# Halved z1 weights kept in DRAM, longer runs of P.V and other PSUM banks in a fused attention and gMLP kernel

## The chip, the cores and the metric

The kernel runs on one core of a Trainium2 chip. The metric is the device time of one execution in microseconds; lower is better. Given are the median of three runs of the kernel before and one profiled execution of it.

## The reference

Two branches read the same normalised input (2048 tokens, 576 features); their product is added to the input.

```python
def _A_ref(x, wqkv, wo):                # 32 heads of 18, causal window of 256
    q, k, v = ...
    scores = einsum("bhqd,bhkd->bhqk", q, k) * Dh ** -0.5
    mask = (i - j >= 0) & (i - j < 256)
    p = softmax(where(mask, scores, -1e9))
    return einsum("bhqk,bhkd->bhqd", p, v)... @ wo

def _B_ref(x, w_in, w_sp, b_sp, w_out): # Fh = 2304
    z = gelu(x @ w_in)
    z1, z2 = z[..., :Fh], layernorm(z[..., Fh:])
    g = einsum("ts,bsf->btf", w_sp, z2) + b_sp[None, :, None]
    return (z1 * g) @ w_out

xn = layernorm(x)
out = x + _A_ref(xn, ...) * silu(_B_ref(xn, ...))
```

## The kernel before, in words

Everything is float32, but TensorE multiplies in a rounded format (float32r). So an operand is *halved*: a high part is a copy by ScalarE (ACT) into float32r, a low part is the rest, by a subtraction on VectorE (DVE) or GpSimd (POOL). A product then takes three matmuls: high by high, high by low, low by high. The 576 input features are nine blocks of 64 rows, so two matmuls of 64 rows each work side by side in the upper and the lower half of TensorE's array; they write the PSUM banks `ma` and `mb`.

The program passes through these stages:

- q, k and v (0 to 195 us of the span). q and k go to `st_d` in DRAM, v to `v_d`.
- z2 (195 to 425 us): 6 pieces of 384 columns (`pc`) by 8 steps of two token tiles (`q`). A step is 27 matmuls in each half; then ACT takes both banks through a gelu into `zt` (four tiles), which SP stores to `z2_d`. Beside it run two generators, advanced once a step: the next piece's weights (fetched by L892 into the tiles named `z1wh` and `z1wl`, halved into `z2w` or into the `att` slots), and `sp_combos`, which loads four blocks of the spatial weights (`a`, L850), makes sums on POOL (L858 to L862) and stores them to `sc_d` (L867).
- The heads (425 to 854 us), and with them z1 = x @ w_z1. For each unit of four heads and half of the tokens there are 32 *maxima* (`max_item`: a matmul of L603 into a bank `sp`, then one DVE operation of L606, which adds the mask `band` and takes the largest score of each query; it is there before the exponentials), and *scores* per key block (`scores`: a matmul of L741 into a bank `tps`, an exponential by ACT into `pt`, and a POOL operation, L753 or L756, that clears what the mask forbids). `pv` multiplies `pt` by v, four heads side by side in parts of 32 columns of the array (L769). What is left of TensorE's time is filled with z1: 18 blocks of 128 columns by two halves by two banks of 27 matmuls (L685).
- The rest of z1 and the product with `wo` (854 to 945 us), the spatial product by a scheme of seven products (945 to 1634), the output product (1634 to 1846).

All DMAs are issued by SP, in one queue. In the heads the order of every engine is written out at build time by a planner: the program keeps a clock with planned costs for each engine, and at each turn asks, for the array's half whose time is behind, whether a run of P.V may go, else a score or a maximum, else a z1 matmul. Between a score and a maximum that could both go, the one whose engine is done first was taken. `SPB` is the number of `sp` banks (3, which leaves 5 - SPB = 2 for `tps`), `PTB` the number of `pt` tiles (5). A run of P.V is begun when its key blocks together hold at least 9 steps of 128 queries, or no `pt` tile is free. The three rules that the change touches read:

```python
return n if size >= 9 or len(pts) >= PTB or not score_queue[0] else 0       # pv_now
return head_ready.get(2 * u + j // 2, 1e9) <= clock and done_max[-SPB] + GUARD <= clock   # can_max
if min(ready)[1]:                                                           # a maximum, else a score
```

The weights of z1 are halved beside the heads. `load_z1` (f is the block of 128 columns) takes the raw block of 576 KB that `fetch_z1` loaded (L646 to L650), and gives three copies to ACT and three subtractions to POOL, which the planner scatters among the z1 matmuls of the block before:

```python
for ks in (slice(0, 3), slice(3, 6), slice(6, 9)):
    jobs.append((partial(act.activation, wh[:, ks], raw[:, ks], AF.Copy), "act", 420))
for ks in (slice(0, 3), slice(3, 6), slice(6, 9)):
    jobs.append((partial(pool.tensor_tensor, wl[:, ks], raw[:, ks], f32(wh[:, ks]), ALU.subtract), "pool", 1000))
```

Of the kernel before, what the change touches and what calls it, by code (L numbers as in the profile page):

```python
# [2 lines left out]

# [13 lines left out]
P = 128  # L17
# [34 lines left out]
WARM = 48  # L52
SPB = 3
PTB = 5

# [10 lines left out]
def kernel(  # L66
# [30 lines left out]
    s_d = dram.tile([S, D], F32, name="s_d")  # L97
    t_d = dram.tile([4, FB, 288], F32, name="t_d")

    ident = const.tile([P, P], F32, name="ident")  # L100
    make_identity(nc, ident)
    band = const.tile([P, 512], F32, name="band")
    pool.memset(band, 0.0)
    pool.memset(band[:, 384:512], NEG)
    pool.affine_select(out=band[:, 0:128], in_=band[:, 0:128], pattern=[[1, 128]], compare_op=ALU.is_gt,
# [131 lines left out]
    with ExitStack() as early:  # L237
# [282 lines left out]
        with ExitStack() as ph:  # L520
# [64 lines left out]
            maxima = {}  # L585
            halved = [aa.tile([P, P], F32R, name=f"ms{i}", bufs=1) for i in range(2)]
            for ms in halved:
                pool.memset(f32(ms), 0.0)

            def max_item(u, j, i):  # L590

                g, half = UNITS[u]
                base = 0 if half == 0 else 6
                if u not in maxima:
                    maxima[u] = aa.tile([P, 4, 8], F32, name="mx")
                mx = maxima[u]
                qb = 8 * half + i
                assert loaded[2 * u + j // 2] == 8
                w = 384 if qb >= 2 else 256
                k0 = (max(qb - 2, 0) - base) * P  # L600
                m0 = {0: 256, 1: 128}.get(qb, 0)
                ps = sps.tile([P, 384], F32, name="sp")
                pe.matmul(ps[:, :w], q_of(u, j)[0:54, i * P:(i + 1) * P], k_of(u, j)[0:54, k0:k0 + w],  # L603
                          start=True, stop=True)
                spend(j % 2, MM * w / 512 + 4)
                dve.tensor_tensor_reduce(out=ps[:, :w], in0=ps[:, :w], in1=band[:, m0:m0 + w], scale=1.0,  # L606
                                         scalar=-3.0e38, op0=ALU.add, op1=ALU.max,
                                         accum_out=mx[:, j, i:i + 1])
                done_max.append(use("dve", 600 if w > 256 else 470))

            def max_split(u):

                mx = maxima.pop(u)
                ms = halved[u % 2][:, 0:64].rearrange("p (a n b) -> p a n b", a=4, n=2)
# [6 lines left out]
            def max_turn(u, r):  # L621

                rs = ROWS[r]
                pt = sps.tile([P, 384], F32, name="sp")
                pe.transpose(pt[:, 0:64], f32(halved[u % 2])[rs], ident[rs, rs])
                spend(r, 80)
                begin = u not in turned
                if begin:
                    turned[u] = aa.tile([64, P], F32, name="mhl")
                m = turned[u]  # L630
# [13 lines left out]

            z1raws = {}

            def fetch_z1(f):
                if f < FH // P and f not in z1raws:
                    z1raws[f] = zw.tile([P, 9, P], F32, name="z1raw", bufs=2)
                    sp.dma_start(z1raws[f], w_z1[f])  # L650

            def load_z1(f):
                fetch_z1(f)
                raw = z1raws[f]
                wh = zw.tile([P, 9, P], F32R, name="z1wh")
                wl = zw.tile([P, 9, P], F32R, name="z1wl")

                jobs = []
                for ks in (slice(0, 3), slice(3, 6), slice(6, 9)):
                    jobs.append((partial(act.activation, wh[:, ks], raw[:, ks], AF.Copy), "act", 420))  # L660
                for ks in (slice(0, 3), slice(3, 6), slice(6, 9)):
                    jobs.append((partial(pool.tensor_tensor, wl[:, ks], raw[:, ks], f32(wh[:, ks]), ALU.subtract),
                                 "pool", 1000))
                return wh, wl, jobs

# [7 lines left out]
            def z1_rows(r):  # L673

                for f in range(FH // P):
                    z1_at[r] = f
                    if f not in z1w:
                        z1w[f] = load_z1(f)
                    wh, wl, jobs = z1w[f]
                    while jobs:  # L680
                        jobs.pop(0)[0]()
                    for b in range(2):
                        ps = fillp.tile([P, 512], F32, name=("ma", "mb")[r])
                        for n, (w, x_) in enumerate(moving_x(wh, wl, slice(b * 512, (b + 1) * 512), r)):
# [10 lines left out]
                            if f + 1 < FH // P and min(z1_at) == f:  # L695
                                if b == 0 and n == 0 and f + 1 not in z1w:
                                    z1w[f + 1] = load_z1(f + 1)
                                if b == 1 and n == 20:
                                    fetch_z1(f + 2)
                                if b == 1 and n % 4 == 2 and f + 1 in z1w and z1w[f + 1][2]:  # L700
                                    job, engine, ns = z1w[f + 1][2].pop(0)
                                    job()
                                    use(engine, ns)
                            yield
# [164 lines left out]
            with ExitStack() as gate:  # L869
# [67 lines left out]
                gz = open_pool(gate, "gz", bufs=2)  # L937
                combos = sp_combos(gate)
                st2 = gz.tile([P, NS, 6, 6], F32, name="st2", bufs=1)
                pairs, z1_first = [], []  # L940
                ahead = [(j, i) for j0 in (0, 2) for i in range(8) for j in (j0, j0 + 1)]
                for pc in range(6):
# [9 lines left out]
                    for q in range(8):  # L952
# [10 lines left out]
                        for h in range(2):  # L963
# [9 lines left out]
                            if pc == 5:  # L973
                                dve.bn_aggr(mv2[:, s, :], st2[:, s].rearrange("p a b -> p (a b)"))
                        if pc == 5 and q == 3:
                            z1w[0] = load_z1(0)
                            fetch_z1(1)
                        if pc == 5 and q == 6:
                            while z1w[0][2]:
                                z1w[0][2].pop(0)[0]()  # L980
                for item in ahead:
                    max_item(0, *item)
                for _ in combos:
                    pass
# [39 lines left out]
            with ExitStack() as heads:  # L1024
# [49 lines left out]
                def pv_now():  # L1074
# [21 lines left out]
                while score_queue[0] or score_queue[1] or todo or filling:  # L1096
# [14 lines left out]
                    if score_queue[r] and can_score(*score_queue[r][0]):  # L1111
                        ready.append((done_exp[-1], 0))
                    if max_queue[r] and can_max(*max_queue[r][0]):
                        ready.append((done_max[-1], 1))
                    if not ready:
# [615 lines left out]
```

## Time and profile before

| | us |
|---|---|
| median of 3 runs (lowest, highest) | 1845.64 (1844.48, 1849.28) |
| the profiled execution | 1847.18 |
| its span, first to last instruction | 1845.3 |
| z2 stage | 195 to 425 |
| first and last z1 matmul | 425.5, 886.5 |
| last run of P.V ends | 852.9 |

The span is what the views of the profile divide up; the execution's own time is 1.9 us longer, and lies 1.5 us above the median. "PEld" is TensorE's weight load, which runs beside the matmuls. A row of waits names who waited, for whom, the sum in us, how often, and the longest. A row of instruction groups gives line, engine, operation, tiles written and read, shapes, count, busy us, mean ns, and the idle time of the engine ahead of them.

### The profile page before, as it was taken

The numbers are of one execution on the slowest core, as the hardware profiler recorded it, in microseconds if no ns is written. First come the engines' busy times: TensorE is split into PE (matmuls) and PEld (weight loads), VectorE is DVE, ScalarE is ACT, GpSimd is POOL, SyncE is SP. The second block draws the span as 40 slices with busy tenths as digits, with TensorE's granted clock in tenths as the row PEclk, the third lists the DMA queues.
The fourth block names the chain that finished last, engine by engine and source line by source line (L and its number), as shares of the span: only waits on it lengthen the run. The fifth ranks groups of instructions, "written<-read, shape, count | busy, mean of one in ns | idle before, by whom it ended". The sixth has DMA issues, their size and how long they took to land.

```text
span 1845.3 us, 37698 instructions
## 1 busy us (share of the span) xinstructions
PE 1822.1 (99%) x14373; PEld 1597.3 (87%) x14373; DVE 1133.8 (61%) x2299; ACT 945.1 (51%) x1757; POOL 430.4 (23%) x509
## 2 busy tenths in 40 slices
PE   8999999999999999999999999999999999999998
PEld 8999999998778777877888888888888888899998
DVE  7321333468777776631156788667886576767876
ACT  5433322225777667774467566465554544544443
POOL 3332333435566456554000000111100000000000
PEclk9999999999999999999999999999999999999999
DMA  8895688888677867645776777789776556796554
GB/s 275 189 234 166 233 279 280 289 265 234 160 194 189 206 176 199 179 140 150 224 244 223 242 239 247 256 291 302 253 256 235 189 188 208 229 269 208 160 162 135
DMA packets 266916, 405.72 MB, mean 220 GB/s; under 512 B 52336, under 2 KB 180592, under 8 KB 266608
## 3 DMA queue, kind: packets, MB, share of 16 engines
q1 hardware_dynamic: 266736, 403.32, 72.0%
q8 instruction: 113, 1.85, 0.4%
q14 instruction: 67, 0.55, 0.1%
HBM read 285.35 MB, written 117.09 MB: 218 GB/s over the span
## 4 chain that ended last, share of the span: by engine, by line
PE 85%; DMA 5%; DVE 5%; ACT 2%; SPq 1%; issue 1%; POOL 0%; DVEq 0%; ACTq 0%; POOLq 0%
PE acc L1470 34%; PE mb L207 11%; PE c L1562 8%; PE ma L685 6%; PE mb L685 6%; PE ma L207 5%; PE ops L769 4%; PE tps L741 3%; PE wops L1189 3%; PE sp L603 3%; DMA st_d<-qkhl 1%; SPq L364 1%; PE mb L381 1%; DMA att<-st_d 1%; DVE spl L117 1%
## 5 line engine op out<-in xcount | busy, mean ns | idle before, releaser
L1470 PE MATMUL acc<-spl,zh 128*128 128x512 f32 x1008 | 392.6, 389 | 0.9 <-DVE spl L117 0.6
L1470 PE MATMUL acc<-sph,zh 128*128 128x512 f32 x1008 | 392.3, 389 | 1.1 <-ACT so L1222 1.1
L1470 PE MATMUL acc<-sph,zl 128*128 128x512 f32 x1008 | 392.2, 389 | 0.0
L606 DVE CUSTOM_DVE_ANT_0 sp<-sp,band 128x384 f32<-128x384 f32 (+1 forms) x512 | 265.0, 566 | 77.4 <-PE sp L603 43.4
L745 ACT ACTIVATE pt<-tps 128x384 f32<-128x384 f32 (+2 forms) x576 | 229.0, 441 | 99.6 <-PE tps L741 74.9
L117 DVE TENSOR_TENSOR spl<-spr,sph 128x1024 fp32r<-128x1024 f32 x168 | 210.2, 1251 | 43.8 <-ACT sph L116 42.8
L685 PE MATMUL mb<-b,z1wh 64*128 64x512 f32 x648 | 225.6, 399 | 0.1
L1470 PEld LDWEIGHTS acc<-spl,zh 128*128 128x128 f32 x1008 | 189.2, 188 | 41.8 <-DVE spl L117 2.6
L1470 PEld LDWEIGHTS acc<-sph,zh 128*128 128x128 f32 x1008 | 189.2, 188 | 40.8 <-ACT so L1222 1.5
L685 PE MATMUL ma<-b,z1wh 64*128 64x512 f32 x648 | 222.8, 401 | 0.4 <-ACT zt L968 0.4
L1470 PEld LDWEIGHTS acc<-sph,zl 128*128 128x128 f32 x1008 | 189.2, 188 | 39.1
L116 ACT ACTIVATE zh<-b 128x384 fp32r<-128x384 f32 x168 | 87.4, 520 | 208.1 <-PE acc L1470 208.0
L116 ACT ACTIVATE sph<-spr 128x1024 fp32r<-128x1024 f32 x168 | 176.0, 1047 | 17.6 <-DMA spr<-in_w_sp_dram 9.2
L117 DVE TENSOR_TENSOR zl<-b,zh 128x384 fp32r<-128x384 f32 x168 | 98.5, 586 | 123.2 <-ACT zh L116 117.8
L741 PE MATMUL tps<-att 56*128 56x384 f32 (+1 forms) x576 | 171.7, 343 | 2.4 <-DMA att<-mhl 1.8
L603 PE MATMUL sp<-att 54*128 54x384 f32 (+1 forms) x512 | 159.5, 349 | 1.3 <-DMA att<-st_d 0.9
L1562 PE MATMUL c<-b,o 128*128 128x288 f32 x1056 | 143.8, 295 | 1.9 <-DVE o L117 1.4
L1562 PEld LDWEIGHTS c<-b,o 128*128 128x128 f32 x1056 | 141.0, 188 | 2.6 <-DVE o L117 1.9
L969 DVE BATCH_NORM_STATS2 st<-zt 128x6 f32<-128x384 f32 x96 | 49.3, 549 | 131.5 <-ACT zt L968 131.3
L685 PE MATMUL ma<-b,z1wl 64*128 64x512 f32 x324 | 128.5, 397 | 0.0
L685 PE MATMUL mb<-b,z1wl 64*128 64x512 f32 x324 | 127.9, 395 | 0.0
L685 PEld LDWEIGHTS mb<-b,z1wh 64*128 64x128 f32 x648 | 117.9, 186 | 6.4 <-ACT z1o L690 1.5
(224 smaller groups left out, 4203.0 us busy)
## 6 DMA issues: line engine op xcount, KB each, us to landing
spr<-sc_d SPq DMA_DIRECT2D x96, 512.0 KB
spr<-in_w_sp_dram SPq DMA_DIRECT2D x72, 512.0 KB
zr<-z_d SPq DMA_DIRECT2D x144, 192.0 KB
z_d<-zt SPq DMA_DIRECT2D x48, 384.0 KB
z_d<-z1o SPq DMA_DIRECT2D x72, 256.0 KB
z1t<-z_d SPq DMA_DIRECT2D x72, 256.0 KB
y_d<-z1t SPq DMA_DIRECT2D x72, 256.0 KB
a<-in_w_sp_dram SPq DMA_DIRECT2D x64, 256.0 KB
```

Of the source, the lines that this page charges most:

```text
L116: act.activation(hi, src, AF.Copy)
L117: dve.tensor_tensor(lo, src, f32(hi), ALU.subtract)
L207: pe.matmul(banks[h][:, :n], *both[h][i], start=i == 0, stop=i == STEPS - 1)
L603: pe.matmul(ps[:, :w], q_of(u, j)[0:54, i * P:(i + 1) * P], k_of(u, j)[0:54, k0:k0 + w], start=True, stop=True)
L606: dve.tensor_tensor_reduce(out=ps[:, :w], in0=ps[:, :w], in1=band[:, m0:m0 + w], scale=1.0, scalar=-3.0e38, op0=ALU.add, op1=ALU.max, accu ...
L685: pe.matmul(ps, w, x_, start=n == 0, stop=n == STEPS - 1)
L741: pe.matmul(ps[:, :m * P], k_of(u, j)[:, (kb - base) * P:(kb - base + 1) * P], q_of(u, j)[:, (a - lo) * P:(a - lo + m) * P], start=True, s ...
L745: act.activation(pt[:, j, d0:d0 + n * P], ps[:, (qa - a) * P:(qa - a + n) * P], AF.Exp, scale=scale)
L769: pe.matmul(o_ps[c][32 * j:32 * j + 32, (qa - 4 * c) * P:(hi - 4 * c + 1) * P], vgs[u][:, kb - k0, j * VW:j * VW + 32], pt[:, j, (qa - kb) ...
L1189: pe.matmul(po[:, i, :288], lt[:, cs], r[:, i * 288:(i + 1) * 288], start=n == 0, stop=n == len(pl) - 1)
L1470: pe.matmul(acc[j], z[:, ps], w[:, cs], start=s == i == 0 and n in OPENS, stop=s == 7 and i == 2, skip_group_check=True)
L1562: pe.matmul(banks[key][:, :288], y, w, start=begin and k == n == 0, stop=close and k == 8 and n == 2, skip_group_check=True)
```

## The change

It has three parts.

1. **z1 weights.** A generator `z1_weights` runs in the z2 stage, 10 times in each piece of 8 steps. In 54 parts of 128 x 384 it loads a third of a raw block (`z1r`, 192 KB, three parts ahead), lets ACT copy and POOL subtract into `z1h` (three tiles), and stores both halves (384 KB) to a new DRAM tensor `z1w_d`. Beside the heads `load_z1` only loads the two halves of a block, 576 KB each. The raw fetches and the halving there are gone.
2. **P.V.** Seven `pt` tiles instead of five, and a run begins at 12 steps instead of 9.
3. **Banks.** Two `sp` banks for maxima instead of three, three `tps` for scores instead of two. A maximum goes ahead of a score wherever both could go. The planned cost of a maximum is 132 ns and one per column (it was 600 or 470), the mask loses its last 128 columns, a maximum over a first key block reads 128 columns instead of 256, and `ms` and `mhl` have one buffer.

```diff
-SPB = 3
-PTB = 5
+SPB = 2
+PTB = 7
...
-                dve.tensor_tensor_reduce(out=ps[:, :w], in0=ps[:, :w], in1=band[:, m0:m0 + w], scale=1.0,
+                w = 384 - m0
+                dve.tensor_tensor_reduce(out=ps[:, :w], in0=ps[:, :w], in1=band[:, m0:384], scale=1.0,
...
-                done_max.append(use("dve", 600 if w > 256 else 470))
+                done_max.append(use("dve", 132 + w))
...
             def load_z1(f):
-                fetch_z1(f)
-                raw = z1raws[f]
-                wh = zw.tile([P, 9, P], F32R, name="z1wh")
-                wl = zw.tile([P, 9, P], F32R, name="z1wl")
...
+                ts = []
+                for i, n in enumerate(("z1wh", "z1wl")):
+                    ts.append(zw.tile([P, 9, P], F32R, name=n))
+                    sp.dma_start(f32(ts[i]), z1w_d[f, i].rearrange("p (k c) -> p k c", k=9))
+                return ts
+
+            def z1_weights(stack):
+                halver = open_pool(stack, "z1p", bufs=3)
+                parts_ = [(f, slice(3 * k, 3 * k + 3), slice(384 * k, 384 * k + 384))
+                          for f in range(FH // P) for k in range(3)]
+                raws_, done = [], []
+
+                def load(n):
+                    if n < len(parts_):
+                        f, ks, _ = parts_[n]
+                        raws_.append(halver.tile([P, 3, P], F32, name="z1r", bufs=4))
+                        sp.dma_start(raws_[-1], w_z1[f][:, ks])
+
+                def store():
+                    n, t = done.pop(0)
+                    f, _, cs = parts_[n]
+                    sp.dma_start(z1w_d[f, :, :, cs].rearrange("n p c -> p n c"), f32(t))
+
+                for n in range(3):
+                    load(n)
+                yield
+                for n in range(len(parts_)):
+                    t = halver.tile([P, 2, 384], F32R, name="z1h")
+                    raw = raws_.pop(0).rearrange("p k c -> p (k c)")
+                    act.activation(t[:, 0], raw, AF.Copy)
+                    pool.tensor_tensor(t[:, 1], raw, f32(t[:, 0]), ALU.subtract)
+                    load(n + 3)
+                    done.append((n, t))
+                    if len(done) > 1:
+                        store()
+                    yield
+                store()
...
+                        for _ in range(1 + (q % 4 == 3)):
+                            next(halving, None)
...
-                        return n if size >= 9 or len(pts) >= PTB or not score_queue[0] else 0
+                        return n if size >= 12 or len(pts) >= PTB or not score_queue[0] else 0
...
-                    if min(ready)[1]:
+                    if ready[-1]:
```

How the program order moves, at the places that matter below. On SP in the z2 stage before, around a step with the next piece's weights (`z1wh` is the weight fetch, `a` and `sc_d` are the spatial blocks and their sums, `z_d<-zt` stores the gelu's output):

```order
L867 DMA sc_d<-a_4112 128x512
L971 DMA z_d<-zt 128x2x384 x2
L892 DMA z1wh<-in_w_z_dram 128x1152
L850 DMA a_4537<-in_w_sp_dram 128x512
L850 DMA a_4539<-in_w_sp_dram 128x512
L850 DMA a_4541<-in_w_sp_dram 128x512
L850 DMA a_4543<-in_w_sp_dram 128x512
L892 DMA z1wl<-in_w_z_dram 128x1152
L971 DMA z_d<-zt 128x2x384 x2
```

The same queue in the same stage now (`z1r` is a third of a raw block, `z1w_d<-z1h` the store of its halves):

```order
L904 DMA z1wh<-in_w_z_dram 128x1152
L984 DMA z_d<-zt 128x2x384 x2
L664 DMA z1r<-in_w_z_dram 128x384
L669 DMA z1w_d<-z1h 128x2x384
L664 DMA z1r<-in_w_z_dram 128x384
L669 DMA z1w_d<-z1h 128x2x384
L879 DMA sc_d<-a_3970 128x512
L879 DMA sc_d<-a_3964 128x512
L879 DMA sc_d<-a_3968 128x512
L879 DMA sc_d<-a_3966 128x512
```

Two or more transfers of the new kind stand in every step between the old ones. On ACT in the same stage, before, the gelus of a step (`zt`) have only the halving of the next piece's weights (`z2w`) between them:

```order
L968 ACTIVATE zt<-ma 128x384
L968 ACTIVATE zt<-mb 128x384
L116 ACTIVATE z2w<-z1wh 128x3x128 x3
L968 ACTIVATE zt<-ma 128x384
L968 ACTIVATE zt<-mb 128x384
```

And now:

```order
L981 ACTIVATE zt<-ma 128x384
L981 ACTIVATE zt<-mb 128x384
L677 ACTIVATE z1h<-z1r 128x384 x2
L117 ACTIVATE z2w<-z1wh 128x3x128 x3
L981 ACTIVATE zt<-ma 128x384
L981 ACTIVATE zt<-mb 128x384
L677 ACTIVATE z1h<-z1r 128x384
```

A copy that needs a landed `z1r` and a stored `z1h` stands between the gelus of every two steps. On TensorE beside the heads, before, a run of P.V (`ops`) with three key blocks, between z1 matmuls (`z1wl`), scores (`tps`) and maxima (`sp`):

```order
L685 MATMUL mb<-b_94,z1wl 128x512
L741 MATMUL tps<-att_2215 128x256
L769 MATMUL ops<-pt,vg 32x128 x4
L769 MATMUL ops<-pt,vg 32x256 x4
L769 MATMUL ops<-pt,vg 32x384 x4
L603 MATMUL sp<-att_2214 128x384
```

A run now, of six blocks:

```order
L703 MATMUL ma<-b_92,z1wl 128x512
L781 MATMUL ops<-pt,vg 32x128 x4
L781 MATMUL ops<-pt,vg 32x256 x4
L781 MATMUL ops<-pt,vg 32x384 x8
L781 MATMUL ops<-pt,vg 32x256 x4
L781 MATMUL ops<-pt,vg 32x128 x4
L603 MATMUL sp<-att_2213 128x384 x2
```

In the whole program the runs of P.V go from 68 to 42, with the same matmuls in them. TensorE's matmuls are the same in number and shape before and after.

More of the change, by code (lines that the diff above doesn't have):

```diff
@@ L2 @@
 from functools import partial
+from itertools import chain
 import concourse.bass as bass
@@ L98 @@
     t_d = dram.tile([4, FB, 288], F32, name="t_d")
+    z1w_d = dram.tile([FH // P, 2, P, 9 * P], F32, name="z1w_d")
     ident = const.tile([P, P], F32, name="ident")
     make_identity(nc, ident)
-    band = const.tile([P, 512], F32, name="band")
+    band = const.tile([P, 384], F32, name="band")
     pool.memset(band, 0.0)
-    pool.memset(band[:, 384:512], NEG)
     pool.affine_select(out=band[:, 0:128], in_=band[:, 0:128], pattern=[[1, 128]], compare_op=ALU.is_gt,
@@ L585 @@
             maxima = {}
-            halved = [aa.tile([P, P], F32R, name=f"ms{i}", bufs=1) for i in range(2)]
-            for ms in halved:
-                pool.memset(f32(ms), 0.0)
+            halved = aa.tile([P, P], F32R, name="ms", bufs=1)
+            pool.memset(f32(halved), 0.0)
             def max_item(u, j, i):
@@ L938 @@
                 combos = sp_combos(gate)
+                halving = z1_weights(gate)
                 st2 = gz.tile([P, NS, 6, 6], F32, name="st2", bufs=1)
@@ L974 @@
                                 dve.bn_aggr(mv2[:, s, :], st2[:, s].rearrange("p a b -> p (a b)"))
+                        for _ in range(1 + (q % 4 == 3)):
+                            next(halving, None)
                         if pc == 5 and q == 3:
                             z1w[0] = load_z1(0)
[L977 to L980, printed above, removed]
                 for item in ahead:
                     max_item(0, *item)
-                for _ in combos:
+                for _ in chain(combos, halving):
                     pass
```

32 lines of the change are left out of this document (6 added, 26 removed).

## The prediction

> **What bounds the kernel now.** I read the engines' busy time first, then the stretches by stage, then the transfers and waits of the stage that gets new work.
>
> ```profile
> PE 1822.1 (99%) x14373; PEld 1597.3 (87%) x14373; DVE 1133.8 (61%) x2299; ACT 945.1 (51%) x1757; POOL 430.4 (23%) x509
> ```
>
> TensorE is busy in 99% of the span, so a change can pay only by shortening its work or its gaps. The next rows give, for each stretch, the busy time of each engine, the granted clock, the share of the 16 DMA engines and GB/s. The first is the z2 stage, the second the heads, the third the rest of the z1 product.
>
> ```profile
> 195.00:425.00 230.00, 229.85 (x2635) 228.07 (x2633) 107.41 (x219) 62.84 (x146) 89.53 (x68) 1.00 0.84 279
> 425.00:854.00 429.00, 424.89 (x4283) 333.14 (x4284) 287.06 (x1055) 295.86 (x735) 244.13 (x355) 1.00 0.71 183
> 854.00:890.00 36.00, 32.68 (x218) 26.24 (x214) 2.32 (x3) 6.57 (x10) 2.00 (x2) 0.98 0.44 132
> ```
>
> In the z2 stage TensorE never waits (229.85 of 230 us), but the DMA engines are 0.84 busy: nowhere else is so little transfer time left. The transfers of that stage, in 40 slices of 5.75 us, then per queue, then by issue:
>
> ```profile
> DMA  5899872999939999699399995659997788797996
> GB/s 167 308 274 373 280 255 111 261 346 374 393 125 295 327 315 342 214 292 315 129 331 317 309 377 167 245 178 269 361 368 281 214 314 236 190 283 238 370 351 263
> DMA packets 34170, 64.16 MB, mean 279 GB/s; under 512 B 3292, under 2 KB 15446, under 8 KB 34142
> ...
> z_d<-zt SPq DMA_DIRECT2D x46, 384.0 KB
> a<-in_w_sp_dram SPq DMA_DIRECT2D x64, 256.0 KB
> sc_d<-a SPq DMA_DIRECT2D x60, 256.0 KB
> z1wh<-in_w_z_dram SPq DMA_DIRECT2D x10, 576.0 KB
> ...
> z1raw<-in_w_z_dram SPq DMA_DIRECT2D x2, 576.0 KB
> ```
>
> 64.16 MB pass in 230 us. No slice moves more than 393 GB/s, and the 22 slices whose digit is 9 average 329. Who waits there now (us, times, longest):
>
> ```profile
> SPq L971 <- ACT zt L968: 80.8, 21, 6.0
> SPq L850 <- DMA sc_d<-a: 9.2, 9, 2.5
> ...
> ACT zt L968 <- PE ma L207: 161.6, 47, 4.8
> ...
> POOL a L858 <- DMA a<-in_w_sp_dram: 120.6, 14, 12.8
> ```
>
> ACT waits for TensorE, SP for ACT: TensorE sets the pace, and transfers follow it with a sixth of their time to spare.
>
> **The change, part by part: the weights through DRAM.** The operations themselves are priced by the rows of the halving that now runs beside the heads, by the gelu that ACT does in the z2 stage, and by one issue on SP:
>
> ```profile
> L702 POOL TENSOR_TENSOR z1wl<-z1raw,z1wh 128x384 fp32r<-128x384 f32 x51 | 50.7, 1013 | 4.1 <-ACT z1wh L702 4.1
> ...
> L702 ACT ACTIVATE z1wh<-z1raw 128x384 fp32r<-128x384 f32 x51 | 26.7, 534 | 0.0
> L850 SPq DMA_DIRECT2D a<-in_w_sp_dram x64: 327/432/1435, 197.1 to 412.8; - x64
> ```
>
> 54 copies on ACT are 54 x 0.534 = 29 us, covered by its 161.6 us of waiting; 54 subtractions on POOL are 54 x 1.013 = 55 us, covered by its 120.6 us; 110 more issues (54 + 54 + 4 - 2) at the median of 0.432 us are 48 us, covered by SP's 80.8 us. If a cover goes, each of these stands in front of something: on ACT the copy stands right behind a pair of gelus and ahead of the next, so an ACT that waits for a raw block or for a free z1h tile frees no PSUM bank, and TensorE stops after one more pair.
>
> The bytes have no such cover. 54 loads of 192 KB are 10.6 MB, 54 stores of 384 KB 21.2 MB; two fetches of 576 KB go (1.2 MB) and four loads of 576 KB come (2.4 MB): 33.0 MB more, 97.2 MB in all. In 230 us that would need 423 GB/s, more than any slice shows. The buffers cannot put it off: raw blocks are fetched three ahead, z1h has three tiles, zt four, and all go through SP in one order. So the stage becomes as long as its transfers. At the best slice, 393 GB/s, 97.2 MB take 247 us (+17); at the mean of the nearly full slices, 329, 295 us (+65). A queue that never runs dry is nearer to the better slices (ten of the 22 are at 342 to 393), but each wait of SP for POOL or ACT leaves a hole; I take 355 GB/s, 274 us: **+44**.
>
> The Trainium skill, "DMA: Bandwidth & Descriptors", Specifications, gives a limit of about 358 GB/s of HBM per core. By it the stage would take 97.2 / 0.358 = 272 us, +42, an estimate from that page; the slices of 361 to 393 stand above it, so here it can hold at most as an average.
>
> Beside the heads the 18 raw fetches become 36 loads. Two of the 18 and four of the 36 lie in the z2 stage:
>
> ```profile
> q1 hardware_dynamic: 64500, 82.50, 68.4%
> ...
> z1raw<-in_w_z_dram SPq DMA_DIRECT2D x16, 576.0 KB
> ```
>
> From 425 to 890 us that is 16 x 0.59 = 9.4 MB more on 82.5, and the share rises from 0.69 to about 0.78. Each block is asked for one block (25 us) ahead, so I cost it at nothing; were that cover gone, each late block would cost a few us.
>
> **The runs of P.V.** Here TensorE changes between two 64-row halves that work side by side and one array with four 32-column parts. A timeline of TensorE (start, us) shows what a change costs:
>
> ```profile
> 652.92 0.28 PE L741 MATMUL tps<-att 56*128 56x256 f32 x1
> 653.13 1.50 PE L769 MATMUL ops<-pt,vg 128*32 128x128 f32 x24
> 654.56 0.38 PE L741 MATMUL tps<-att 56*128 56x256 f32 x1
> ...
> 852.04 0.50 PE L685 MATMUL ma<-b,z1wl 64*128 64x512 f32 x1
> 852.04 0.49 PE L685 MATMUL mb<-b,z1wl 64*128 64x512 f32 x1
> 852.47 0.43 PE L769 MATMUL ops<-pt,vg 128*32 128x128 f32 x8
> 852.82 0.50 PE L685 MATMUL ma<-b,z1wh 64*128 64x512 f32 x1
> ...
> 853.16 0.40 PE L685 MATMUL ma<-b,z1wh 64*128 64x512 f32 x1
> ...
> 853.40 0.39 PE L685 MATMUL ma<-b,z1wl 64*128 64x512 f32 x1
> ```
>
> A pair of z1 matmuls starts every 0.24 us (853.16 to 853.40). Ahead of the run it takes 0.43 (0.19 more), behind it 0.34 (0.10 more). The run with one step of 128 queries holds TensorE 0.35 us, one with six steps (key blocks of 128, 256 and 384 queries by the program order) 1.43; so a step is 0.216 and 0.13 is fixed. Together 0.42 us a run. In program order the runs go from 68 to 42, with the same matmuls in them: 26 x 0.42 = **-11**.
>
> **Banks and the order of maxima.** What TensorE's weight loads wait for in the heads:
>
> ```profile
> PEld tps L741 <- ACT pt L745: 3.7, 12, 0.7
> ...
> PEld ops L769 <- ACT pt L745: 3.2, 9, 0.4
> PEld sp L603 <- DVE mx L606: 3.1, 7, 1.1
> ...
> PEld ops L769 <- POOL pt L753: 0.7, 3, 0.3
> ```
>
> A third bank for exponentials, and an ACT and a POOL that lose 29 and 55 us of halving there, can win at most about the first, second and fourth: -8. Two banks for maxima can lose more than the 3.1 us shown:
>
> ```profile
> 562.60 0.60 DVE L606 CUSTOM_DVE_ANT_0 sp<-sp,band 128x384 f32<-128x384 f32 x1
> ...
> 563.11 0.60 DVE L606 CUSTOM_DVE_ANT_0 sp<-sp,band 128x384 f32<-128x384 f32 x1
> ...
> 563.62 0.60 DVE L606 CUSTOM_DVE_ANT_0 sp<-sp,band 128x384 f32<-128x384 f32 x1
> ```
>
> Back to back VectorE takes a maximum every 0.51 us, which is what the new cost of 132 + 384 ns says (it was 600). With maxima first, TensorE is given them at just that pace, and with two banks each hiccup of DVE reaches it. If each of some 460 maxima cost 0.04 us that is +18. Between -8 and +18 I take 0, as the waits shown are of 3 us on either side. The 32 maxima of a first key block that now read 128 columns instead of 256, the smaller mask and the single ms tile change only DVE or POOL time that nothing waits for: 0.
>
> **The sum.** The profiled execution took 1847.2 us (span 1845.3), 1.5 above the median of the runs. 1847.2 + 44 - 11 + 0 = 1880; on the median's footing **1879 us**. A measurement of this kernel tells about 0.3% (5.5 us) from no change.
>
> **The rivals.**
> - *The transfers fit after all.* Then the z2 stage stays at 230 us and the runs' 11 us are kept: about 1835, faster. It decides at 97.2 / 241 = 403 GB/s: at that average the stage's loss equals the gain. For it speak the slice of 393 and that loads and stores might overlap better in a full queue; against it that the 22 busy slices average 329. Chance 0.10. The Trainium skill names, on the same page and section, a fabric ceiling of 435 GB/s; by that, 97.2 MB would take 223 us, an estimate, and this rival would hold. No slice here comes near it.
> - *A tie.* Transfers at 393 throughout (+17) and the most from the heads (-11 - 8): 1844. Chance 0.06.
> - *Worse: the chain and the banks.* SP, ACT and POOL now wait in one order, so the stage falls to the mean of the busy slices (+65), and two banks cost the heads their 18 us: 1846 + 65 - 11 + 18 = 1918. For it: SP already waits nine times for sc_d stores; against: when SP is held, transfers behind the late one still run. Chance 0.16, from about 1905 up.
> - *The forecast*, 1855 to 1905: 0.68.
>
> The two outermost cases hold about 2 in 10 outside 1847 to 1914, which is the range; the forecast's own is 1855 to 1905. Faster 0.10, within 0.3% 0.06, slower 0.84.
>
> **What would show it.** The z2 stage, 230 us now, ends some 44 us later against its start; its DMA share is above 0.95 and its rate 340 to 370 GB/s; TensorE's gaps there end on ACT's zt, and ACT's own on DMA into z1r or out of z1h. From the first z1 matmul to its last, 464 us now, it is about 453. If the z2 stage holds 230 to 240 us, my bound on the rate is wrong; if waits of sp for mx exceed 10 us, the zero for the banks is.

## The result and the profile after

| | median of 4 runs, us | lowest, highest | span of the profiled execution |
|---|---|---|---|
| before | 1846.49 | 1844.48, 1849.28 | 1845.3 |
| after | 1922.28 | 1920.46, 1925.46 | 1920.4 |

The ratio is 1.0411 with a 95% interval of 1.0391 to 1.0431. The change costs 76 us where 33 were forecast: the direction was right, the size was not. The first rows of the page of after, its granted clock and its DMA share:

```profile
PE 1842.0 (96%) x14373; PEld 1606.8 (84%) x14373; DVE 1147.6 (60%) x2299; ACT 938.1 (49%) x1757; POOL 433.8 (23%) x507
...
PEclk9999999998999999999999999999999999999999
...
DMA  8895999997877677674487776778886655687554
```

TensorE is busy for 1842.0 us, 20 more than before with the same matmuls (the clock was lower in places), and idle for 78 where it was idle for 23. The stretches (columns as in the prediction: busy time of PE, PEld, DVE, ACT and POOL, granted clock, DMA share, GB/s) say where:

```profile
196.00:430.00 234.00, 215.72 (x2330) 211.16 (x2327) 93.31 (x135) 80.31 (x185) 131.79 (x109) 0.95 1.01 357
430.00:478.00 48.00, 30.64 (x298) 28.77 (x298) 25.15 (x85) 5.39 (x13) 15.26 (x13) 0.82 0.81 258
478.00:923.00 445.00, 420.39 (x4190) 324.12 (x4190) 290.88 (x1054) 264.74 (x680) 192.33 (x303) 0.97 0.72 195
923.00:966.00 43.00, 42.36 (x310) 34.00 (x306) 2.00 (x3) 7.18 (x11) 0.00 (x0) 0.99 0.51 160
```

The first two rows are the z2 stage, the third the heads up to the last run of P.V, the fourth the rest of z1. In the z2 stage the DMA engines are full and TensorE is not; in the heads the DMA engines are 0.72 busy, and TensorE still stands idle for 24.6 us of 445. From the first and last matmul of each kind the two executions divide like this (us):

| | first z2 matmul to first z1 matmul | first z1 matmul to last of the product with `wo` | from there to the end |
|---|---|---|---|
| before | 230.0 | 519.3 | 900.4 |
| after | 282.1 | 542.4 | 900.0 |
| difference | +52.1 | +23.1 | -0.4 |

I call the first column the z2 stage and the second the heads below. The transfers from 196 to 478 us of after, in 40 slices of 7 us:

```profile
DMA  7999999999999999999999999999999997989990
GB/s 192 380 294 382 379 376 343 337 403 365 392 309 383 383 363 352 382 366 323 390 389 373 373 389 384 364 336 395 303 400 348 370 294 199 241 266 349 347 378 11
DMA packets 56499, 95.89 MB, mean 340 GB/s; under 512 B 5004, under 2 KB 37772, under 8 KB 56468
```

And the waits in the same stretch (who, for whom; us, times, longest):

```profile
ACT z1h L677 <- DMA z1w_d<-z1h: 109.4, 27, 8.6
...
ACT zt L981 <- PE ma L208: 39.4, 13, 7.1
...
PE ma L208 <- ACT zt L981: 16.7, 8, 4.7
...
PE sp L603 <- POOL a L873: 12.8, 1, 12.8
```

The order of causes has turned round. ACT waited 161.6 us for TensorE before; now it waits 109.4 us until a store lets a z1h tile go, and TensorE waits for ACT's gelu. The longest single wait of TensorE is at the end of the stage: 12.8 us for a sum of the spatial blocks on POOL, which ran late with the transfers. In the heads (478 to 923 us):

```profile
POOL ou L830 <- DMA rp<-r_d: 28.1, 5, 11.3
...
POOL ou L830 <- DMA att<-st_d: 21.4, 2, 15.4
...
PEld sp L603 <- DVE mx L607: 12.1, 43, 2.3
...
PE tps L753 <- DMA att<-mhl: 8.7, 2, 6.2
...
PE ops L781 <- POOL pt L765: 3.3, 1, 3.3
```

Of these, before showed from 425 to 854 us:

```profile
POOL ou L818 <- DMA att<-st_d: 2.0, 1, 2.0
PE tps L741 <- DMA att<-mhl: 1.8, 1, 1.8
POOL ou L818 <- DMA rp<-r_d: 1.7, 2, 1.1
```

They have grown five- to sixteenfold, and all but the one for `mx` end on a small transfer or on POOL, which itself waits for such transfers. One can be followed whole. SP's timeline (start, us it takes to issue) around the loads of a z1 block, then all that touches the tile `mhl` from 636 to 651 us, then TensorE's row behind the wait (in brackets the idle time before it and what ended it):

```profile
632.63 0.35 SPq L650 DMA_DIRECT2D z1wh<-z1w_d  x1
633.08 0.38 SPq L650 DMA_DIRECT2D z1wl<-z1w_d  x1
...
638.92 0.30 SPq L826 DMA_DIRECT2D rp<-r_d  x1
642.56 0.29 SPq L551 DMA_DIRECT2D att<-st_d  x1
```

```profile
SPq L551 <- DMA z1wl<-z1w_d: 3.3, 1, 3.3
```

```profile
L638 SPq DMA_DIRECT2D att<-mhl x4: 610/618/644, 645.7 to 649.1; - x4
L632 DVE COPY mhl<-sp x2: 206/212/217, 637.6 to 637.8; 64x64 f32<-64x64 f32 x2
```

```profile
650.42 1.26 PE L753 MATMUL tps<-att 56*128 56x384 f32 x3 [6.16 <-DMA att<-mhl]
```

The hole in SP's timeline from 639.2 to 642.6 us is its wait of 3.3 us (second fence) for the z1wl load issued at 633.08. The trace's semaphores say why SP waits for it: the DMAs of these kernels use eight semaphores in turn, and none is issued before the one that used its semaphore last, as a rule eight places ahead, has landed. The `att<-st_d` of 642.56 has the semaphore of the z1wl load, which landed at 642.54, 9.5 us after its issue. The maxima `mhl` were ready at 638.0 us, but their transfer, further back in SP's program order, is issued only from 645.7 on. The scores need it, and TensorE stands for 6.16 us. Right around it, from 647.3 to 654.1 us, TensorE's clock record stands at half. From 190 to 1020 us after has 12 such stretches, 3.4 or 6.8 us long and one of 13.7, where before has 2; in the 3.4 us ahead of each of them TensorE was idle for 1.5 to 3.0 us. Over the whole execution TensorE worked 52 us at half clock in after and 11.5 in before. Half of the difference is 20 us, which is what its busy time grew by, so a wait of a few us is paid twice: once as idle time, once as slow matmuls. The Trainium skill, "TensorE: Matmul & The Clock Gate", Part 1, says that the clock is gated in windows of 3413 ns by how busy TensorE was; the lengths seen here agree with one, two and four windows.

### The profile page after: what moved, and what is told of

Its sections match the earlier page's. It is cut to its first block, busy times and chain, and to the rows that moved or that the text cites. A ratio compares the mean times of both kernels' runs of the same rounds, so it can differ in the third digit from the quotient of the medians.

```text
span 1920.4 us, 37901 instructions
## 1 busy us (share of the span) xinstructions
PE 1842.0 (96%) x14373; PEld 1606.8 (84%) x14373; DVE 1147.6 (60%) x2299; ACT 938.1 (49%) x1757; POOL 433.8 (23%) x507
## 4 chain that ended last, share of the span: by engine, by line
PE 68%; DMA 18%; DVE 5%; SPq 3%; issue 2%; ACT 2%; POOL 1%; DVEq 0%; ACTq 0%; POOLq 0%
PE acc L1481 33%; PE c L1573 8%; PE ma L703 6%; PE mb L703 5%; PE ops L781 4%; PE ma L208 3%; DMA z1w_d<-z1h 3%; PE sp L603 3%; PE mb L208 3%; DMA z_d<-zt 2%; PE tps L753 2%; DMA a<-in_w_sp_dram 1%; DMA att<-st_d 1%; DMA rp<-r_d 1%; SPq L365 1%
## 5 line engine op out<-in xcount | busy, mean ns | idle before, releaser
L607 DVE CUSTOM_DVE_ANT_0 sp<-sp,band 128x384 f32<-128x384 f32 (+2 forms) x512 | 269.0, 546 | 105.2 <-PE sp L603 87.0
L757 ACT ACTIVATE pt<-tps 128x384 f32<-128x384 f32 (+2 forms) x576 | 214.4, 448 | 55.8 <-PE tps L753 36.7
L703 PE MATMUL ma<-b,z1wh 64*128 64x512 f32 x648 | 231.4, 407 | 3.7 <-ACT z1o L708 3.1
L603 PE MATMUL sp<-att 54*128 54x384 f32 (+1 forms) x512 | 181.6, 382 | 24.1 <-POOL a L873 12.8
L753 PE MATMUL tps<-att 56*128 56x384 f32 (+1 forms) x576 | 164.4, 338 | 8.8 <-DMA att<-mhl 8.7
L603 PEld LDWEIGHTS sp<-att 54*128 54x128 f32 x512 | 91.6, 188 | 60.4 <-POOL a L873 15.5
L208 PE MATMUL ma<-z2w,b 64*128 64x384 f32 x648 | 125.0, 347 | 8.1 <-ACT zt L981 8.1
```

What stands on the lines that cost most here:

```text
L208: pe.matmul(banks[h][:, :n], *both[h][i], start=i == 0, stop=i == STEPS - 1)
L703: pe.matmul(ps, w, x_, start=n == 0, stop=n == STEPS - 1)
L753: pe.matmul(ps[:, :m * P], k_of(u, j)[:, (kb - base) * P:(kb - base + 1) * P], q_of(u, j)[:, (a - lo) * P:(a - lo + m) * P], start=True, s ...
L757: act.activation(pt[:, j, d0:d0 + n * P], ps[:, (qa - a) * P:(qa - a + n) * P], AF.Exp, scale=scale)
```

## The experiments

Each expectation was written with the medians then known; the tables' stages are those of one profiled execution each. Such an execution lies up to 5.2 us from its kernel's median (nohalv_later 5.2 and nohalv_onlyhigh 4.0 above, nohalv_actload 4.8 below), so a few us between the stages of two kernels say little by themselves.

**z1only: part 1 by itself.** The changed kernel with the old P.V rule and the old banks:

```diff
-SPB = 2
-PTB = 7
+SPB = 3
+PTB = 5
...
-                        return n if size >= 12 or ...
+                        return n if size >= 9 or ...
...
-                    if ready[-1]:
+                    if min(ready)[1]:
```

> The changed kernel with only its first part: z1 weights through DRAM; P.V at 9 steps and five pt tiles, three sp banks, the old costs and the old choice between maximum and score. Theory A (late transfers: the heads lose because the z1w_d loads share SP's queue and the DMA engines): z2 stage +52 us as in the changed kernel, heads still +20, about 1918 us. Theory B (the order: the heads lose because of two sp banks, maxima first and long runs): z2 stage +52, heads 0, about 1898 us.

Measured: 1905.1 us, ratio 1.0331 (1.0312 to 1.0351); z2 stage 275.6, heads 534.9. Part 1 makes 45.6 of the 52.1 us in the z2 stage, and it adds 15.6 to the heads, where I had it at nothing. That lies between the two theories, nearer to the first. Its transfers from 196 to 430 us:

```profile
DMA packets 50140, 84.61 MB, mean 362 GB/s; under 512 B 4382, under 2 KB 33950, under 8 KB 50114
```

**banksonly: part 3 on the kernel before.**

```diff
-SPB = 3
+SPB = 2
...
-                done_max.append(use("dve", 600 if w > 256 else 470))
+                done_max.append(use("dve", 132 + w))
...
-                    if min(ready)[1]:
+                    if ready[-1]:
```

> The kernel before with only the third part: two sp and three tps banks, maxima first, cost 132 + w, the small mask, one ms and mhl. Theory A: within 5 us of before, 1846 us. Theory B: the heads lose here what they lose in the changed kernel, some 15 to 30 us, 1862 to 1876 us, with waits of sp for mx above 10 us.

Measured: 1853.04 us, ratio 1.0046 (1.0032 to 1.0061); z2 stage 233.9, heads 520.7. The 3.9 us in the z2 stage come at its end, where the first 32 maxima stand among the last z2 matmuls: they begin at 397.1 us in both kernels, and the last one starts at 426.2 us here and at 422.4 in before. TensorE's weight loads wait longer there for a bank that the maximum has left (from 395 us to the stage's end, of this kernel and then of before):

```profile
PEld sp L601 <- DVE mx L605: 4.4, 4, 1.2
```

```profile
PEld sp L603 <- DVE mx L606: 1.7, 5, 0.4
```

**nobytes: the change without its bytes.** All 54 copies on ACT and all 54 subtractions on POOL stay, but only the first block is loaded and stored; the others' operands are the tiles of that block, and every load beside the heads reads block 0. It leaves out 51 loads and 51 stores, and z1 is made from wrong weights.

```diff
-                    if n < len(parts_):
+                    if n < 3:
...
+                        raws_.append(fixed[n % 3])
...
                 def store():
                     n, t = done.pop(0)
+                    if n > 2:
+                        return
```

> The changed kernel, but only the first of 18 blocks is loaded raw and stored halved; the other 51 parts repeat ACT's copies and POOL's subtractions on the same raw tiles without any transfer, and the heads load the first block's halves 18 times (so z1 is computed from the wrong weights; traffic in the heads unchanged). If the bytes bound the z2 stage: it falls back to 230 to 235 us, total about 1870. If the chain of ACT and POOL work between the gelus bounds it: it stays at 270 to 280 us, total about 1920.

Measured: 1875.04 us, ratio 1.0163 (1.0147 to 1.0178); z2 stage 233.9, heads 545.0. The z2 stage is that of banksonly to 0.1 us. Its stretch and ACT's longest wait from 196 to 430 us:

```profile
196.00:430.00 234.00, 229.78 (x2633) 227.87 (x2629) 118.21 (x219) 84.23 (x197) 146.94 (x121) 1.00 0.84 281
```

```profile
ACT zt L985 <- PE ma L208: 139.1, 46, 5.6
```

With the work on ACT and POOL in place and the bytes gone, TensorE is full again and ACT waits for it as before. So the cover that I claimed for ACT and POOL holds, and the stage's loss comes with the transfers, all but the banks' 3.9 us and 2.6 that I could not attribute (282.1 - 275.6 - 3.9). The 102 issues are gone from SP as well, so this run does not test SP's cover; by the trace of after, SP's instructions take 156 of the 234 us, so there is room for them. The heads' loss is still whole: it has another cause.

**nohalv_noloads and nohalving: which part of part 1 costs the heads.** Both halve only the first block in the z2 stage, all blocks of z1 are made from its weights, and parts 2 and 3 stay. nohalv_noloads also loads only two blocks beside the heads and uses their tiles over again; nohalving loads all 18, always from block 0. First nohalv_noloads, of which nohalving leaves the line pair with `f > 1` out:

```diff
             def load_z1(f):
+                if f > 1:
+                    return z1w[f - 2]
...
-                          for f in range(FH // P) for k in range(3)]
+                          for f in range(1) for k in range(3)]
```

> The changed kernel without halving in the z2 stage beyond the first block, and in the heads only the first two blocks' halves are loaded, then used again (z1 from the wrong weights). Order on TensorE in the heads as in the changed kernel. Theory A: z2 stage 230, the heads at the 11 us gain that was forecast, about 1835 us. Theory B: z2 stage 230, the heads still lose 23 us, about 1870 us.

> The changed kernel with only the first block halved in the z2 stage; the heads load that block's halves 18 times (z1 from the wrong weights), so their traffic and order are as in the changed kernel. Against the run without loads it adds 32 loads of 576 KB and nothing else. If those loads are what the heads lose: z2 stage 234 us, from the first z1 matmul to the end of wo 540 to 545 us, about 1872 us. If the loss needs the ACT and POOL work of the halving ahead of the heads: 516 us there, about 1846 us.

Measured: 1845.79 us, ratio 1.0005 (0.9994 to 1.0016), heads 516.1 without the loads (3.2 less than before, where 11 were forecast); 1871.41 us, ratio 1.0135 (1.0112 to 1.0158), heads 539.9 with them. The 32 loads of 576 KB are the difference: 23.8 us of the heads' time, 25.6 us between the medians. From the first z1 matmul to the last one, without and with loads:

```profile
430.00:892.00 462.00, 454.17 (x4495) 351.79 (x4496) 292.85 (x1057) 269.89 (x690) 192.44 (x303) 0.99 0.62 161
```

```profile
429.00:915.00 486.00, 462.95 (x4494) 358.48 (x4493) 293.23 (x1055) 271.88 (x690) 192.38 (x303) 0.98 0.71 193
```

TensorE's idle time grows by 15.2 us (7.8 to 23.0) and its busy time by 8.8 with the same matmuls. The DMA share only goes from 0.62 to 0.71. What waits in the second (430 to 870 us):

```profile
POOL ou L830 <- DMA rp<-r_d: 44.6, 6, 13.6
...
PE tps L753 <- DMA att<-mhl: 4.4, 1, 4.4
PE sp L603 <- DMA att<-st_d: 3.4, 2, 2.9
...
PE ops L781 <- POOL pt L768: 2.9, 1, 2.9
```

The first two of these without the loads (430 to 848 us):

```profile
POOL ou L832 <- DMA rp<-r_d: 15.5, 6, 8.9
...
PE tps L755 <- DMA att<-mhl: 0.9, 1, 0.9
```

POOL waits 15.5 us for `rp` in a kernel that loses nothing, so POOL's row alone does not tell what TensorE loses. SP waits at the loads themselves too (nohalving, 428 to 880 us):

```profile
SPq L650 <- PE tps L753: 6.5, 13, 1.2
SPq L650 <- PE sp L603: 4.5, 5, 3.4
SPq L650 <- PE mb L703: 3.4, 5, 2.0
```

There are two tiles for high halves and two for low ones, so the load of a block cannot go before TensorE is done with the block two places earlier, and SP stands there with all that is behind it. In before the raw fetch (L650 there) shows no such wait for TensorE.

**Three theories of how the loads do it.** A load of 576 KB might hold the queue (then smaller pieces help), the bytes might slow everything (then half the bytes cost half), or POOL might be planned to want `rp` too early (then a later due time helps). Each kernel is nohalving with one edit. nohalv_pieces loads a block in six pieces of 192 KB, one at every eighth matmul; nohalv_onlyhigh loads only the high half after the second block, and z1 uses an old low half; nohalv_later moves the due times of the division that waits for `rp`.

```diff
+                    for k in range(0, 9, 3):
+                        parts_.append(partial(sp.dma_start, f32(ts[i][:, k:k + 3]), z1w_d[0, i][...]))
...
+                                if n % 8 == 4 and f + 1 in z1w and z1w[f + 1][2]:
+                                    z1w[f + 1][2].pop(0)()
```

> As the run without halving, but the two loads of 576 KB per block are cut into six of 192 KB, given to SP one by one over the z1 matmuls of the block before. Same bytes, more issues. Theory C (a large load holds up what SP issues behind it: late rp, mhl and st_d transfers, then waits of TensorE and half clock): the heads recover, 515 to 525 us instead of 545, about 1848 us. Theory D (the DMA engines have too many bytes): still about 1870 us.

```diff
+                    if i and f > 1:
+                        ts.append(z1w[f - 2][1])
+                        continue
```

> As the run without halving, but after the second block only the high half is loaded (576 KB once a block, as the raw fetch was before); the low half is that of two blocks earlier. Theory C: one large load a block costs what it cost before, little: 518 to 525 us, about 1849 us. Theory D: half of the loss, about 1858 us.

```diff
-MAX_NS = 5000
+MAX_NS = 9000
...
-DIVIDE_AT = (28000, 29200, 30400, 31600, 37000, 38000, 39000, 40000)
+DIVIDE_AT = (36000, 37200, 38400, 39600, 45000, 46000, 47000, 48000)
```

> As the run without halving (both loads of 576 KB a block kept), but the planner's due times are 8 us later for the division of the outputs (DIVIDE_AT) and 4 us later for the scores of a unit after its maxima were moved (MAX_NS 9000). Same bytes. If more bytes cost the heads because rp and mhl land after the times the planned order counts on, so that POOL and TensorE stand waiting in program order: waits of POOL's division on rp fall from 45 us to under 20, the heads go from 540 to about 525 us, total about 1856 us. If the cost lies elsewhere: still 1871 us.

| | bytes loaded for z1 | heads, us | median, us | ratio (95%) |
|---|---|---|---|---|
| nohalv_noloads | 0 | 516.1 | 1845.79 | 1.0005 (0.9994 to 1.0016) |
| nohalv_onlyhigh | half | 529.8 | 1853.97 | 1.0041 (1.0022 to 1.0060) |
| nohalving | all | 539.9 | 1871.41 | 1.0135 (1.0112 to 1.0158) |
| nohalv_pieces | all | 539.4 | 1867.72 | 1.0105 (1.0073 to 1.0136) |
| nohalv_later | all | 543.6 | 1870.77 | 1.0141 (1.0108 to 1.0174) |

The first three rows from the first z1 matmul to the last, per queue (packets, MB, share of 16 engines' time), in the order none, half, all:

```profile
q1 hardware_dynamic: 61992, 73.78, 61.2%
```

```profile
q1 hardware_dynamic: 64508, 83.40, 66.3%
```

```profile
q1 hardware_dynamic: 66607, 92.66, 70.2%
```

So in these executions 9.6 MB cost 13.7 us and 18.9 MB cost 23.8: 1.3 to 1.4 us per MB, at shares of 0.66 and 0.70. By the medians it is 8.2 and 25.6 us, 0.9 and 1.4 us per MB. Half of the bytes thus cost between a third and a little over half of the loss, and 1853.97 lies between theory C (1849) and theory D (1858), so this run does not decide between them. Smaller pieces change nothing in the stages and at most a few us in the medians (the intervals overlap; the profiled execution, 1870.90 us, is one of the longer ones): the large load that holds SP, which the timeline of after shows, is one way to lose the time, and without it most of the time is lost all the same. The waits of nohalv_pieces, and those of nohalv_later:

```profile
PE tps L761 <- DMA att<-mhl: 8.7, 6, 3.7
PE ops L789 <- POOL pt L776: 6.5, 1, 6.5
```

```profile
POOL pt L765 <- DMA z1wl<-z1w_d: 23.0, 1, 23.0
PEld sp L603 <- DVE mx L607: 21.7, 77, 4.4
...
PEld ma L703 <- ACT z1o L708: 6.3, 4, 2.9
```

The later division did what it was meant to: the wait of 44.6 us for `rp` is gone. The time stayed, in other waits. That theory fell too.

**nohalv_actload: the loads off SP's queue.** nohalving with the loads issued by ACT:

```diff
-                    sp.dma_start(f32(ts[i]), z1w_d[0, i]...)
+                    act.dma_start(f32(ts[i]), z1w_d[0, i]...)
```

> As the run without halving (both loads of 576 KB a block), but ACT issues these loads instead of SP; same bytes at the same place of the program. If the heads lose because SP's queue stands behind the large loads: 516 to 525 us from the first z1 matmul to the end of wo, about 1852 us. If they lose because the bytes slow all transfers: 540 us or more, 1870 us or more (ACT now waits for the loads' tiles too).

Measured: 1896.34 us, ratio 1.0282 (1.0262 to 1.0303); heads 560.3, 20 us worse. TensorE now waits for ACT's exponentials (428 to 880 us):

```profile
PE tps L753 <- ACT pt L757: 20.0, 7, 6.4
```

This run does not separate SP's queue from the bytes. ACT's loads take their turn among the same eight semaphores: SP's issue at 605.28 us waits for a load that ACT issued at 597.52, and ACT stands idle ahead of a load for up to 5.2 us (723.0 to 728.2). It shows only that the loads cost still more when ACT issues them.

**Parts 2 and 3 without the loads.** Part 2 could not be put on the kernel before, since seven `pt` tiles do not fit beside the raw z1 tiles; pv6 is as near as it goes: six tiles, runs from 12 steps, one raw tile fewer (58 runs instead of 68).

```diff
-PTB = 5
+PTB = 6
...
-                    z1raws[f] = zw.tile([P, 9, P], F32, name="z1raw", bufs=2)
+                    z1raws[f] = zw.tile([P, 9, P], F32, name="z1raw", bufs=1)
...
-                        return n if size >= 9 or ...
+                        return n if size >= 12 or ...
```

> The kernel before with the second part alone as far as memory allows: six pt tiles, runs of P.V at 12 steps, one raw z1 tile instead of two, the smaller mask, one ms and mhl; three sp banks and the old choice stay. The runs of P.V go from 68 to 58. At 0.42 us a run: -4 us, 1841 us. If a longer run costs on ACT or VectorE what it saves on TensorE: within 2 us of before.

Measured: 1848.24 us, ratio 1.0005 (0.9993 to 1.0016), heads 521.7: no gain from ten runs fewer, at a later raw fetch. The other three kernels are nohalv_noloads (same weights left out) with the old P.V rule, the old banks, or both:

```diff
# noloads_plain: SPB = 3, PTB = 5, size >= 9, min(ready), old costs
# noloads_pv:    SPB = 3, PTB = 7, size >= 12, min(ready), old costs
# noloads_banks: SPB = 2, PTB = 5, size >= 9
```

> No halving beyond the first block and no z1 loads after the second (z1 from the wrong weights), with P.V and banks as in the kernel before: the base for the next two. 65 runs of P.V. z2 stage 230 us, heads to the end of wo 512 to 518 us, total about 1841 us.

> As that base, with seven pt tiles and runs at 12 steps: 51 runs of P.V. At 0.42 us a run 14 x 0.42 = 6 us less: about 1835 us. If the longer run costs elsewhere what it saves: as the base.

> As that base, with the third part: two sp and three tps banks, maxima first. 75 runs of P.V, so +4 us in the heads from the runs, +4 in the z2 stage from the maxima at its end, and what the two banks cost: about 1850 us, weight loads of sp waiting some 10 us for mx instead of 3.

| | runs of P.V | banks | heads, us | median, us | ratio (95%) |
|---|---|---|---|---|---|
| noloads_plain | 65 | old | 512.5 | 1837.76 | 0.9961 (0.9948 to 0.9974) |
| noloads_pv | 51 | old | 510.7 | 1837.89 | 0.9969 (0.9949 to 0.9988) |
| noloads_banks | 75 | new | 520.8 | 1851.63 | 1.0041 (1.0026 to 1.0057) |
| nohalv_noloads | 42 | new | 516.1 | 1845.79 | 1.0005 (0.9994 to 1.0016) |

With the old banks the new P.V rule is worth 1.8 us of the heads for 14 runs, and nothing by the medians; with the new banks 4.7 us for 33 runs, 5.8 by the medians, and there the intervals do not overlap. That is between nothing and 0.18 us a run. The banks cost 8.3 us of the heads with the old P.V rule and 5.4 with the new one. noloads_plain also says what dropping the raw loads and the halving beside the heads is worth by itself: 519.3 - 512.5 = 6.8 us, a gain I had not put in the sum. Beside the new banks it is worth nothing: banksonly has 520.7, noloads_banks 520.8. In that kernel the wait for maxima is as in banksonly's heads (428 to 850 us):

```profile
PEld sp L603 <- DVE mx L607: 13.1, 49, 0.9
```

## Why the prediction was right or wrong

The heads' 23.1 us by the runs, in one order of taking the steps: -6.8 (no raw loads, no halving), +3.6 (P.V and banks together, 512.5 to 516.1), +23.8 (the loads of halved weights), +2.5 (not explained; nobytes, whose z2 stage is short, has 545.0, so the scatter of one execution is at least as large). With +52.1 and the start 0.5 us later, -0.4 for the rest, that is, but for rounding, the 75.1 us between the spans.

- **The z2 stage at +44: right in its mechanism and nearly in its size.** Part 1 alone measured +45.6, the whole change +52.1. The share is 1.01 from 196 to 430 us, TensorE waits there for ACT's `zt`, as forecast. ACT waits for stores out of z1h (109.4 us); loads into z1r barely show. The mean of 357 GB/s up to 430 us is my 355; over the whole stage it is 340, as the last 48 us ran at 258. The Trainium skill's limit of about 358 ("DMA: Bandwidth & Descriptors", Specifications) agrees with the 357 as an average, while slices here reach 403. What I left out lies at the end of the stage: 3.9 us of banks, and 2.6 more that no run attributes.
- **"Each block is asked for one block (25 us) ahead, so I cost it at nothing": the step that failed, by 24 us.** Asking for a block early protects the block, and no wait of TensorE for a z1 block is in the heads of after. It does not protect the small transfers that stand behind it in SP's order and on the same 16 engines: `mhl`, `rp`, `att`. I had looked for lateness only in the thing that was loaded. How their delay becomes 24 us stays open (below). I also read a share of 0.78 (0.77 by the rows that I gave) as room; in a stage whose order is fixed, the loads cost about 1.3 us per MB at a share of 0.70. The sign that I named fell with it: from the first z1 matmul to the last it is 487.9 us, not 453, and before it was 461.2, not 464.
- **"26 x 0.42 = -11": over-sized at least twofold.** Between nothing and 0.18 us a run is what came back, at most 6 us for 33 runs. Of the 0.42, 0.13 was the run's own fixed part and 0.29 what I read at its two borders in one timeline; what was seen again is nearer to the first alone. Why the border's part does not come back I did not test. Part of it shows where the time lies: against the first z1 matmul, nohalv_noloads ends its last run 4.1 us later than noloads_banks, and the z1 left behind it takes 8.7 us less; the heads' own work did not get shorter, more z1 fitted into it.
- **The zero for the banks: wrong, +3.9 in the z2 stage and +1.4 (on the kernel before), +5.4 or +8.3 (without the loads) in the heads.** The sign I set for it came: TensorE's weight loads of `sp` wait 12.1 us for `mx`, more than the 10 I named. The bound of +18 was not reached.
- **The covers on ACT and POOL in the z2 stage: right.** nobytes keeps that work and costs the stage nothing beyond the banks. No run tests SP's cover; the trace of after leaves it room.
- **The rival "Worse"** was at 1918, near the time, but for other reasons: its +65 measured 52, its +18 measured 5 to 12, and the missing 24 us are the loads that it had at nothing as well.

What stays open is why 18.9 MB cost 24 us while the DMA engines are 0.70 busy. The size of a load, one due time and the issuing engine were each changed, and none of them brought the time back; only fewer bytes did. A reading that fits is that the transfers take longer, that the order of all engines was planned without that, and that whichever engine stands at a late transfer passes the wait on. It is not shown. From issue to landing, by the semaphores in the traces (460 to 845 us), `rp` took 3.8 us in the mean without the loads and 4.6 with them (nohalving), `att<-st_d` 4.6 and 5.0, `z_d<-z1o` 4.2 and 5.2, but `mhl` 2.3 in both. Before has 4.4, 5.1, 4.2 and 3.7 and does not lose the time, so longer transfers alone do not explain it. Two further causes were not tested: that no more than eight DMAs are under way at once, and SP's 14 us of waiting at the loads for a free tile. A plan made with the longer transfers in it was not tried either.

None of these kernels that makes all of z1 from its own weights is faster than before. noloads_plain shows what could be had if the halved weights cost nothing to bring: 8 us.

## What to carry to other kernels

Before bytes are moved into a stage, read the stage's DMA share and rate as a budget: at a share of 0.84 this one moved 279 GB/s, full it moved 357, and half as many bytes again made it 46 us longer. A prefetch that is early for its own consumer can still cost the stage that it runs in, so in a stage with a fixed order count it in us per MB, here 0.9 to 1.4 at shares of 0.66 to 0.70, and do not stop at the share. A saving read at the borders of one instruction run is an upper bound until a kernel with fewer runs has been timed.

## What the runs showed of the hardware

- At a DMA share of 1.01 (after) and 1.02 (z1only), the transfers, loads and stores mixed and 1.7 KB a packet in the mean (84.61 MB in 50140, z1only), ran at 357 and 362 GB/s over 234 us; no slice of 7 us of after passed 403.
- Short waits were followed by half clock: 12 half-rate stretches of 3.4 to 13.7 us between 190 and 1020 us in after, 2 in before, 9 in z1only, none in banksonly, in after and before each behind 3.4 us with 1.5 to 3.0 us of idle time. TensorE's busy time rose by 20 us with the same matmuls, which is half of the additional 41 us that it worked at half clock.
- Six loads of 192 KB cost the heads the same as two of 576 KB (539.4 and 539.9 us, in one execution each; the medians differ by 3.7 us, with overlapping intervals).
